# How the reciprocal deviations get from tokens' rows to output rows: two VectorE turns and four small transfers a group, in place of a TensorE product

## The chip, the core and the metric

The kernel runs on one core of a Trainium2 chip. The metric is device microseconds of one execution. The core's engines work from queues of their own, each in the order of the program: TensorE (PE; its weight loads are listed as PEld), VectorE (DVE), ScalarE (ACT), GpSimd (POOL) and SyncE (SP), which here only issues DMA transfers. ScalarE and GpSimd issue some transfers too. A name with a q behind it (SPq, ACTq) is the engine's sequencer: waits and issues.

## The reference

Two blocks, one after the other. The first filters a sequence in the frequency domain; the second is a feed-forward block with SoLU and a layer norm, all in float32:

```python
X = np.fft.rfft(x, axis=1)                      # x: (8, 3136, 256)
y = np.fft.irfft(X * (filt_r + 1j * filt_i), n=3136, axis=1)
t = y.reshape(25088, 256)
h = t @ w_in                                    # (25088, 1024)
e = np.exp(h - h.max(-1, keepdims=True))
solu = h * e / (e.sum(-1, keepdims=True) + 1e-9)
mu = solu.mean(-1, keepdims=True)
var = ((solu - mu) ** 2).mean(-1, keepdims=True)
out = ((solu - mu) / np.sqrt(var + 1e-6) * g_ln) @ w_out
```

What matters here is the factor 1 / sqrt(var + 1e-6): one number for each of the 25,088 tokens, which multiplies the token's output row.

## The kernel before

**Tiling.** The tokens are cut into 196 blocks of 128, two blocks make a pair (98 pairs), two pairs a group (49 groups of 4 blocks). The loop at the end runs `step(k)` for k = 0 to 204; an even k and the odd one behind it belong to pair j = k // 2. A step holds one block's work in each of several stages, so that the engines work on different blocks at once: the hidden product (`product`, L799, seven products for a pair of blocks instead of eight, with sums of blocks made by GpSimd), its evacuation by ScalarE (`keep`, L809) and VectorE (`finish`, L823 and L820), two and three steps later the exponential (L833), the normalization (L845), the turn (L863) and the variance (L853), and some five pairs later the output product (`project`, L935) and its scaling (`keep_out`, L951 on ScalarE; `finish_out`, L955 on VectorE). The Fourier transforms of the next batch elements are spread over the same steps: rows of x are loaded three steps ahead (L270), multiplied (L294, L326, L396), and go through DRAM between.

**Order.** Everything is inside `tc.manual_schedule()`: each engine runs its instructions in the order in which `step` issues them. Semaphores are set by the framework.

**Turn and regroup.** The output product needs the hidden dimension on the partitions. VectorE's transpose works on squares of 32x32. `turn(k)` (L863) transposes a block's 128x1024 in such squares, and `regroup(p, i)` (L880) moves 32-row strips of four turned blocks together with four transfers of 128 KB on SyncE's queue, into the tile `solu_t`. By this the tokens come out in another order: the token at partition 32a + i of block b of a group is row 32b + i of output tile a.

**The factor's way.** ScalarE leaves the four blocks' variances in a tile of 128 x 4. `deviations(g)`, at step k = 4g + 6, computes rs = (var + floor) ** -0.5 on GpSimd (L890, L891). This has the token's partition 32a + i on the rows and the block b in the columns, and must become row 32b + i, column a. So GpSimd also writes `wide` (L893), a 128 x 128 tile in which each rs stands in the column of its place in the square of 32, and at k = 4g + 8 `regroup_deviations` lets TensorE multiply it by a table of 128 x 4 that picks the square (L899), into a corner of a PSUM bank that the output product of the pair before is using (`places`). ScalarE copies the 128 x 4 result to `rs_t` (L902). The first use of it is `keep_out` at k = 4g + 9, then `finish_out`, for the two pairs of the group.

**Queues.** On SyncE, an even step k issues eight transfers of `regroup` (pair j - 3: four for each half), then two stores of output rows (L963), then, in the stages with row loads, four loads of x (L270). `regroup`'s second half reuses the buffer of the pair two before, which TensorE must have read for the last time (`project(p, 4)` in the same step).

Of the kernel before, what the change touches and what calls it, by code (L numbers as in the profile page):

```python
# [9 lines left out]
FP32 = mybir.dt.float32  # L10
# [3 lines left out]
ALU = mybir.AluOpType  # L14
# [4 lines left out]
P = 128  # L19
# [89 lines left out]
def kernel(  # L109
# [10 lines left out]
    nc = tc.nc  # L120
# [6 lines left out]
    de_dram = nc.inline_tensor(de_host, name="de_tbl").ap()  # L127
    there_dram = nc.inline_tensor(
        np.ascontiguousarray(de_host[:, :, 0].reshape(NP, P, P).transpose(1, 0, 2)), name="there_tbl").ap()
    one_dram = nc.inline_tensor(np.eye(P, dtype=np.float32), name="one_tbl").ap()  # L130
    rows = np.arange(P)[:, None]
    turn_dram = nc.inline_tensor(np.concatenate(
        [rows % 32 == np.arange(32), rows // 32 == np.arange(4)], 1).astype(np.float32),
        name="turn_tbl").ap()

    def pool(name, bufs, space=None, stack=ctx):
        kw = {} if space is None else {"space": space}
# [5 lines left out]
    small = pool("sm", 4)  # L143
# [15 lines left out]
    neg_half, floor_sb = small_consts[:, 0:4], small_consts[:, 4:5]  # L159
# [278 lines left out]
    with ExitStack() as st:  # L438
# [145 lines left out]
        for i0, n, rows in ((0, 4, P), (4, 4, P), (8, NP - 9, P), (NP - 1, 1, NQ)):  # L584
            f, at = filters[i0]
# [91 lines left out]
    def psum(name):  # L677
        return ps_t.tile([P, 2, C], FP32, name=name, tag="t")
# [15 lines left out]
    pools["de"] = pool("de1", 2)  # L694
    spread = pool("spread", 1)
    turn_t = spread.tile([P, 36], FP32, name="turn_t", tag="turn_t")
    second.pools = pools
    for c, at, n, kind, dims in (
            (0, 0, 4 * C, "t2", "p (v c) -> p v c"), (0, 4 * C, 4 * C, "f", "p (v k c) -> p v k c"),
# [188 lines left out]
    def deviations(g):  # L888
        rs = small.tile([P, 4], FP32, name=f"rs_{g}", tag="rs", bufs=2)
        nc.gpsimd.tensor_tensor(out=rs, in0=variances.pop(g), in1=floors.pop(g), op=ALU.add)  # L890
        nc.gpsimd.tensor_tensor(out=rs, in0=rs, in1=neg_half, op=ALU.pow)  # L891
        spreads[g] = wide = spread.tile([P, 4, 32], FP32, name=f"wide_{g}", tag="wide")
        nc.gpsimd.tensor_tensor(  # L893
            out=wide, in0=turn_t[:, 0:32].rearrange("p (o i) -> p o i", o=1).broadcast_to([P, 4, 32]),
            in1=rs.rearrange("p (b o) -> p b o", o=1).broadcast_to([P, 4, 32]), op=ALU.mult)

    def regroup_deviations(g, ps):

        nc.tensor.matmul(out=ps, lhsT=spreads.pop(g).rearrange("p b i -> p (b i)"), rhs=turn_t[:, 32:36],  # L899
                         start=True, stop=True)  # L900
        rss[g] = small.tile([P, 4], FP32, name=f"rs_t_{g}", tag="rs_t")
        nc.scalar.copy(out=rss[g], in_=ps)  # L902

    def project_sums(p, step):

# [146 lines left out]
    def step(k):  # L1052
        j, odd = divmod(k, 2)
        p = j - (LAG - 1) // 2 if odd else j - (LAG + 1) // 2
        if not 0 <= p < pairs:
            p = None
        hid, proj = k < blocks, p is not None
        sums_of_x = differences[k] + products[k]
        if not odd and k > LAG:
            for job in sums_of_x:  # L1060
                job()
            sums_of_x = []
        if not odd and 2 <= j - 4 < pairs:
            project_sums(j - 4, 0)
        if k < LAG:
            if not odd:
                product(j, 1)
                keep(j, k, 0)
                product(j, 2)
                finish(j, k, 0, (k, 0), 1)  # L1070
            else:
                product(j, 5)
                keep(j, k - 1, 1)
                finish(j, k, 1, (k - 1, 1), 2)
        for job in top[k] + (sums_of_x + stores[k] if k < LAG else stores[k] + sums_of_x):
            job()
        if not odd and 0 <= j - 4 < 2:
            project_sums(j - 4, 0)
        if odd and j + 1 < pairs:
            pair_sums(j + 1)  # L1080
        if not odd:
            if hid and k > LAG:
                product(j, 1)
                keep(j, k, 0)
            if 2 <= k < blocks:
                exponential(k - 2)
            if proj:
                project(p, 5)
                keep_out(p, 1, (1, 1) if p in last else (0, 1))
            if p in last:  # L1090
                keep_out(p, 0, (0, 1))
                finish_out(p, 1, 1, (1, 1), 1)
            if blocks <= k < blocks + 2:
                exponential(k - 2)
            if hid and k > LAG:
                product(j, 2)
            if 3 <= k < blocks + 3:
                turn(k - 3)
            if hid and k > LAG:
                finish(j, k, 0, (k, 0), 1)  # L1100
            if proj and p not in last:
                finish_out(p, 1, 1, (0, 1), 1)
            for job in early[k]:
                job()
            if 3 <= k < blocks + 3:
                square(k - 3)
            if hid:
                product(j, 6)
                keep(j, k + 1, 0)
            if proj:  # L1110
                project(p, 3)
                if p not in last:
                    keep_out(p, 0, (0, 1))
                project(p, 4)
            if j >= 4 and j % 2 == 0 and j - 4 < pairs:
                regroup_deviations((j - 4) // 2, places.pop(p) if proj else psum("ps_rs")[:, 0, 0:4])
            for job in spectrum_loads[k]:
                job()
            if 0 <= j - 3 < pairs - 2:
                regroup(j - 3, 0)  # L1120
                regroup(j - 3, 1)
            elif j - 3 == pairs - 2:
                regroup(j - 3, 1, nc.scalar.dma_start, range(2))
                regroup(j - 3, 0)
                regroup(j - 3, 1, parts=range(2, 4))
                regroup(j - 2, 0)
                regroup(j - 2, 1, parts=range(2))
            if 0 <= j - 4 < pairs:
                project_sums(j - 4, 1)
            if j - 3 == pairs - 2:  # L1130
                regroup(j - 2, 1, nc.gpsimd.dma_start, range(2, 4))
            if 0 <= j - 3 < pairs and j % 2:
                deviations((j - 3) // 2)
            if hid:
                product(j, 7)
            if p in last:
                finish_out(p, 0, 1, (0, 1), 2)
                finish_out(p, 1, 0, (1, 0), 1)
                store_out(p)
            if 2 <= k < blocks + 2:  # L1140
                normalize(k - 2)
            for job in second_parts[k] + middle[k] + first_parts[k]:
                job()
            if proj and p not in last:
                finish_out(p, 1, 0, (1, 0), 1)
                store_out(p)
        else:
            if hid and k >= LAG:
                product(j, 5)
                keep(j, k - 1, 1)  # L1150
                finish(j, k, 1, (k - 1, 1), 2)
            for job in early[k]:
                job()
            if proj:
                project(p, 1)
                keep_out(p, 0, (0, 0))
                project(p, 2)
                finish_out(p, 0, 0, (0, 0), 1)
            if 2 <= k < blocks + 2:
                exponential(k - 2)  # L1160
            if hid:
                product(j, 3)
                product(j, 4)
            if proj:
                project(p, 6)
                project(p, 7)
            for job in second_parts[k] + middle[k]:
                job()
            if 3 <= k < blocks + 3:
                turn(k - 3)  # L1170
            if hid:
                finish(j, k - 1, 1, None, 0)
                finish(j, k, 0, (k, 0), 2)
            if 2 <= k < blocks + 2:
                normalize(k - 2)
            if proj:
                keep_out(p, 1, (1, 0))
            if 3 <= k < blocks + 3:
                square(k - 3)
            for job in first_parts[k]:  # L1180
                job()
        if k < 3:
            convert_w_out(k + 1)
        if k == 2:
            prepare_w_out(0)
        if k == 4:
            prepare_w_out(1)
        if 5 <= k < 9:
            prepare_w_out(k)
        for job in late[k] + loads[k]:  # L1190
            job()
        if k < 4:
            scale_w_out(k)

    with tc.manual_schedule():
        pair_sums(0)
        nc.gpsimd.dma_start(out=turn_t, in_=turn_dram)
        for load in first_loads:
            load()
        nc.vector.tensor_scalar(out=g_sb, in0=g_sb, scalar1=-1.0 / SHRINK, scalar2=None, op0=ALU.mult)  # L1200
        convert_w_out(0)
        for k in range(blocks + LAG):
            step(k)
# [30 lines left out]
```

## Time and profile before

| | |
|---|---|
| median of 3 runs | 1576.14 us (1568.17 to 1578.04) |
| the profiled execution | 1569.28 us, span 1567.5 us |
| granted TensorE clock, mean | 0.996 |
| PE busy | 1532.5 us (98%), 12844 matmul passes |
| DVE busy | 1254.9 us (80%) |
| POOL busy | 1157.2 us (74%) |
| ACT busy | 927.9 us (59%) |
| DMA, share of 16 engines: SyncE's queue, GpSimd's, ScalarE's | 42.5%, 18.6%, 7.2% |

A float32 product is carried out in two passes, so 49 products L899 are 98 matmul passes and 98 weight loads. A line of the profile's groups gives line, engine, operation, out<-in by the program's names, shape and count, and behind the bar the busy time and the mean of one in ns. In the views by time the first number is the start in us from the start of the span, the second the length; merged instructions carry a count (x8). `[0.75 <-ACT rs_t L902]` means that the engine was idle for 0.75 us before, and that ScalarE's instruction of line 902 ended this. The transfers are busiest up to 1200 us (DMA share 0.71 to 0.81 in the stretches of 120 to 300, 300 to 600, 600 to 1060 and 1060 to 1200 us) and quiet behind (0.43 from 1200 to 1520 us), when no Fourier work is left.

### The profile page before, as it was taken

The numbers are of one execution on the slowest core, as the hardware profiler recorded it, in microseconds if no ns is written. First come the engines' busy times: TensorE is split into PE (matmuls) and PEld (weight loads), VectorE is DVE, ScalarE is ACT, GpSimd is POOL, SyncE is SP. The second block draws the span as 40 slices with busy tenths as digits, with TensorE's granted clock in tenths as the row PEclk, the third lists the DMA queues.
The fourth block names the chain that finished last, engine by engine and source line by source line (L and its number), as shares of the span: only waits on it lengthen the run. The fifth ranks groups of instructions, "written<-read, shape, count | busy, mean of one in ns | idle before, by whom it ended". The sixth has DMA issues, their size and how long they took to land.

```text
span 1567.5 us, 36719 instructions
## 1 busy us (share of the span) xinstructions
PE 1532.5 (98%) x12844; PEld 1061.7 (68%) x12844; DVE 1254.9 (80%) x2233; ACT 927.9 (59%) x1898; POOL 1157.2 (74%) x1346
## 2 busy tenths in 40 slices
PE   8988999999999999999999999999999999999997
PEld 5633576667666776667766776667776777777777
DVE  4879878897998789878998698877998777776773
ACT  3565655666556656666566655666556666666663
POOL 2578886697879678887779767786766767676665
PEclk9999999999999999999999999999999999999999
DMA  9768788877987689667886588766874545343434
GB/s 246 252 202 226 218 225 220 227 212 207 252 242 204 173 236 254 196 173 192 249 230 190 152 229 247 203 184 176 233 204 119 138 122 135 88 115 102 116 104 118
DMA packets 342256, 298.07 MB, mean 190 GB/s; under 512 B 27915, under 2 KB 311573, under 8 KB 342073
## 3 DMA queue, kind: packets, MB, share of 16 engines
q1 hardware_dynamic: 278872, 175.82, 42.5%
q0 software_dynamic: 29568, 87.33, 18.6%
q10 hardware_dynamic: 33634, 32.58, 7.2%
q8 instruction: 104, 1.70, 0.5%
q14 instruction: 78, 0.64, 0.1%
HBM read 118.02 MB, written 74.84 MB: 123 GB/s over the span
## 4 chain that ended last, share of the span: by engine, by line
PE 59%; DMA 2%; DVE 0%; SPq 0%; issue 0%; POOL 0%; ACT 0%; ACTq 0%; POOLq 0%
PE o L935 26%; PE m L799 26%; PE py L396 2%; PE pc L326 1%; PE pa L294 1%; PE pb L326 1%; DMA solu_t<-turn 1%; DMA x<-in_x_dram 0%; SPq L880 0%; DMA out_dram<-ot 0%; PE o L899 0%; POOL u L778 0%; ACT e L833 0%; DVE h L845 0%; DVE h L820 0%
## 5 line engine op out<-in xcount | busy, mean ns | idle before, releaser
L935 PEld LDWEIGHTS o<-w_out_sb,solu_t 128*128 128x128 f32 x3136 | 381.1, 192 | 47.3 <-issue 43.5
L799 PE MATMUL m<-w_in_sb,s 128*128 128x512 f32 x784 | 398.4, 609 | 5.8 <-ACT h L809 3.3
L935 PE MATMUL o<-w_out_sb,solu_t 128*128 128x128 f32 x3136 | 400.2, 276 | 1.7 <-DVE ot L955 1.6
L935 PEld LDWEIGHTS o<-w_out_sb,u 128*128 128x128 f32 x2352 | 306.4, 191 | 138.3 <-issue 108.6
L799 PE MATMUL m<-w_in_sb,y 128*128 128x512 f32 x588 | 307.8, 607 | 5.6 <-DVE nmax L823 3.8
L935 PE MATMUL o<-w_out_sb,u 128*128 128x128 f32 x2352 | 309.6, 275 | 2.6 <-POOL u L778 1.8
L845 DVE SCALAR_TENSOR_TENSOR h<-e,h 128x1024 f32<-128x1024 f32 x196 | 308.7, 1575 | 0.4 <-ACT e L833 0.4
L951 ACT ACTIVATE ot<-o,rs_t 128x128 f32<-128x128 f32 x392 | 143.6, 367 | 248.2 <-PE o L935 246.1
L809 ACT COPY h<-m 128x512 f32<-128x512 f32 x294 | 173.2, 589 | 195.6 <-PE m L799 191.0
L778 POOL TENSOR_TENSOR u<-solu_t 128x512 f32<-128x512 f32 x98 | 135.0, 1377 | 184.7 <-DMA solu_t<-turn 126.2
L823 DVE CUSTOM_DVE_ANT_0 h<-m,h 128x512 f32<-128x512 f32 x196 | 134.3, 685 | 165.4 <-ACT h L809 103.1
L853 ACT ACTIVATE h<-h,nmu 128x1024 f32<-128x1024 f32 x196 | 225.1, 1148 | 53.4 <-DVE turn L863 53.4
L863 DVE STREAM_TRANSPOSE turn<-h 128x1024 f32<-128x1024 f32 x196 | 243.0, 1240 | 3.8 <-DVE ot L955 0.3
L833 ACT ACTIVATE e<-h,nmax 128x1024 f32<-128x1024 f32 x196 | 225.3, 1149 | 8.1 <-DVE h L845 6.6
L778 POOL TENSOR_TENSOR u<-solu_t,u 128x512 f32<-128x512 f32 x98 | 136.0, 1388 | 94.0 <-PE o L935 93.4
L799 PEld LDWEIGHTS m<-w_in_sb,s 128*128 128x128 f32 x784 | 127.9, 191 | 90.9 <-issue 71.6
L955 DVE SCALAR_TENSOR_TENSOR ot<-o,rs_t,ot 128x128 f32<-128x128 f32 x299 | 103.7, 347 | 97.0 <-ACT ot L951 59.8
L778 POOL TENSOR_TENSOR u<-u,solu_t 128x512 f32<-128x512 f32 x98 | 161.9, 1652 | 15.9 <-PE o L935 9.0
L799 PEld LDWEIGHTS m<-w_in_sb,y 128*128 128x128 f32 x588 | 96.7, 191 | 102.1 <-issue 46.2
L778 POOL TENSOR_TENSOR solu_t<-solu_t,solu_t 128x512 f32<-128x512 f32 x98 | 155.0, 1581 | 0.9
L778 POOL TENSOR_TENSOR s<-y 128x128 f32<-128x128 f32 x196 | 100.2, 511 | 6.1 <-DMA x<-in_x_dram 5.7
L396 PEld LDWEIGHTS py<-wb_t,t 50*64 50x64 f32 x3584 | 57.6, 135 | 42.9 <-issue 18.7
(121 smaller groups left out, 1953.9 us busy)
## 6 DMA issues: line engine op xcount, KB each, us to landing
solu_t<-turn SPq DMA_DIRECT2D x780, 128.0 KB
out_dram<-ot SPq DMA_DIRECT2D x196, 128.0 KB
t<-d POOLq DMA_DIRECT2D x112, 200.0 KB, 6.8
d<-x POOLq DMA_DIRECT2D x100, 200.0 KB, 5.3
t<-d ACTq DMA_DIRECT2D x37, 512.0 KB
f<-f_dram POOLq DMA_DIRECT2D x37, 512.0 KB, 7.6
d<-g POOLq DMA_DIRECT2D x36, 512.0 KB, 5.0
x<-in_x_dram SPq DMA_DIRECT2D x112, 98.0 KB
```

What stands on the lines that cost most here:

```text
L396: nc.tensor.matmul(out=views[g][64 * h:64 * h + 64, cb, i, :], lhsT=t4[rows, i, c0:c0 + 64], rhs=wb_t[rows, 0:N1], start=True, stop=True)
L778: nc.gpsimd.tensor_tensor(out=out, in0=in0, in1=in1, op=op)
L799: nc.tensor.matmul(out=ms[j, bank], lhsT=lhsT, rhs=w_in_sb[:, w, :], start=m in (1, 2, 7), stop=True, skip_group_check=True)
L809: nc.scalar.copy(out=h_half(k, i), in_=ms[j, 0])
L823: nc.vector.tensor_tensor_reduce(out=h_half(k, i), in0=ms[j, bank], in1=h_half(*kept), scale=1.0, scalar=sofar, op0=ALU.add, op1=ALU.min, ...
L833: nc.scalar.activation(out=e, in_=hs[k], func=AFT.Exp, bias=nmaxs.pop(k)[:, 1:2], scale=-1.0, accum_out=esums[g][:, i:i + 1])
L845: nc.vector.scalar_tensor_tensor(out=solu, in0=e, scalar=SHRINK, in1=solu, op0=ALU.mult, op1=ALU.mult, accum_out=nmu)
L853: nc.scalar.activation(out=solu, in_=solu, func=AFT.Square, bias=nmu, scale=-float(DFF), accum_out=variances[g][:, i:i + 1])
L863: nc.vector.transpose(out=turns[g][:, :, i, :], in_=solus[k].rearrange("p (f j) -> p f j", j=32))
L935: nc.tensor.matmul(out=pos[p, bank], lhsT=lhs[:, f, :], rhs=w[:, f, :], start=f == 0 and (m in (1, 2, 7) or alone), stop=True, skip_group_ ...
L951: nc.scalar.activation(out=out_half(p, *to)[0], in_=pos[p, 0], func=AFT.Copy, scale=rs)
L955: nc.vector.scalar_tensor_tensor(out=ot, in0=pos[p, bank], scalar=rs, in1=out_half(p, *kept)[0], op0=ALU.mult, op1=ALU.add)
```

## The change

The product by TensorE goes, but for the last group. GpSimd now writes rs into the first four columns of a tile `lines` of 128 x 32. At the end of step 4g + 7 VectorE turns `lines` in its squares of 32, in place: rs of block b and square a then lies along row 32a + b. Four transfers on SyncE's queue move these rows, four rows of 32 numbers (128 bytes) each, to the rows a, 32 + a, 64 + a, 96 + a of `corners`, and at the end of step 4g + 8 VectorE turns `corners` in place: row 32b + i, column a holds what is wanted. `corners` has two halves, one for even and one for odd groups; `lines` is one buffer. Both are set to zero once at the start. The last group (g = 48) still uses `wide`, the product and ScalarE's copy. A constant table's place in DRAM moves as well.

```diff
+    lines = small.tile([P, 32], FP32, name="lines", tag="lines", bufs=1)
+    corners = spread.tile([P, 2, 32], FP32, name="corners", tag="corners")
...
     def deviations(g):
...
-        nc.gpsimd.tensor_tensor(out=rs, in0=rs, in1=neg_half, op=ALU.pow)
-        spreads[g] = wide = spread.tile([P, 4, 32], FP32, name=f"wide_{g}", tag="wide")
-        nc.gpsimd.tensor_tensor(
-            out=wide, in0=turn_t[:, 0:32].rearrange("p (o i) -> p o i", o=1).broadcast_to([P, 4, 32]),
-            in1=rs.rearrange("p (b o) -> p b o", o=1).broadcast_to([P, 4, 32]), op=ALU.mult)
+        nc.gpsimd.tensor_tensor(out=lines[:, 0:4], in0=rs, in1=neg_half, op=ALU.pow)
+
+        if 2 * g == pairs - 2:
+            spreads[g] = wide = pools["diff"].tile([P, 4, 32], FP32, name=f"wide_{g}", tag="diff")
+            nc.gpsimd.tensor_tensor(
+                out=wide, in0=turn_t[:, 0:32].rearrange("p (o i) -> p o i", o=1).broadcast_to([P, 4, 32]),
+                in1=lines[:, 0:4].rearrange("p (b o) -> p b o", o=1).broadcast_to([P, 4, 32]), op=ALU.mult)
+
+    def product_deviations(g, ps):
...
-        rss[g] = small.tile([P, 4], FP32, name=f"rs_t_{g}", tag="rs_t")
+        rss[g] = corners[:, g % 2, 0:4]
         nc.scalar.copy(out=rss[g], in_=ps)
+
+    def regroup_deviations(g):
+
+        places = corners[:, g % 2, :]
+        nc.vector.transpose(out=lines, in_=lines)
+        for a in range(4):
+            nc.sync.dma_start(out=places[a:P:32, :], in_=lines[32 * a:32 * a + 4, :])
+
+    def place_deviations(g):
+
+        rss[g] = places = corners[:, g % 2, :]
+        nc.vector.transpose(out=places, in_=places)
...
-            if j >= 4 and j % 2 == 0 and j - 4 < pairs:
-                regroup_deviations((j - 4) // 2, places.pop(p) if proj else psum("ps_rs")[:, 0, 0:4])
+            if k == blocks + 4:
+                product_deviations(pairs // 2 - 1, places[p])
...
+        if k >= 7 and k % 4 == 3 and k - 3 < blocks:
+            regroup_deviations((k - 7) // 4)
+        if k >= 8 and k % 4 == 0 and k - 4 < blocks:
+            place_deviations((k - 8) // 4)
         if k < 3:
             convert_w_out(k + 1)
...
+        nc.gpsimd.memset(lines, 0.0)
+        nc.gpsimd.memset(corners, 0.0)
```

The two new calls stand at the end of a step, behind its evacuations, normalization and spectrum products and ahead of `late[k]` and of the step's loads.

More of the change, by code (lines that the diff above doesn't have):

```diff
@@ L129 @@
         np.ascontiguousarray(de_host[:, :, 0].reshape(NP, P, P).transpose(1, 0, 2)), name="there_tbl").ap()
-    one_dram = nc.inline_tensor(np.eye(P, dtype=np.float32), name="one_tbl").ap()
     rows = np.arange(P)[:, None]
@@ L134 @@
         name="turn_tbl").ap()
+    one_dram = nc.inline_tensor(np.eye(P, dtype=np.float32), name="one_tbl").ap()
     def pool(name, bufs, space=None, stack=ctx):
@@ L890, in deviations @@
         nc.gpsimd.tensor_tensor(out=rs, in0=variances.pop(g), in1=floors.pop(g), op=ALU.add)
-        nc.gpsimd.tensor_tensor(out=rs, in0=rs, in1=neg_half, op=ALU.pow)
-        spreads[g] = wide = spread.tile([P, 4, 32], FP32, name=f"wide_{g}", tag="wide")
-        nc.gpsimd.tensor_tensor(
-            out=wide, in0=turn_t[:, 0:32].rearrange("p (o i) -> p o i", o=1).broadcast_to([P, 4, 32]),
-            in1=rs.rearrange("p (b o) -> p b o", o=1).broadcast_to([P, 4, 32]), op=ALU.mult)
-    def regroup_deviations(g, ps):
-        nc.tensor.matmul(out=ps, lhsT=spreads.pop(g).rearrange("p b i -> p (b i)"), rhs=turn_t[:, 32:36],
+        nc.gpsimd.tensor_tensor(out=lines[:, 0:4], in0=rs, in1=neg_half, op=ALU.pow)
[5 more added lines that the diff above has]
+    def product_deviations(g, ps):
+        wide = spreads.pop(g)
+        nc.tensor.matmul(out=ps, lhsT=wide.rearrange("p b i -> p (b i)"), rhs=turn_t[:, 32:36],
                          start=True, stop=True)
-        rss[g] = small.tile([P, 4], FP32, name=f"rs_t_{g}", tag="rs_t")
+        rss[g] = corners[:, g % 2, 0:4]
         nc.scalar.copy(out=rss[g], in_=ps)
+    def regroup_deviations(g):
[6 more added lines that the diff above has]
+        nc.vector.transpose(out=places, in_=places)
     def project_sums(p, step):
```

## The prediction

> **What bounds the kernel.** I read the chain of work that ended last first, since it says on which engine a saved microsecond shortens the run. By engine (shares of the span):
>
> ```profile
> PE 59%; DMA 2%; DVE 0%; SPq 0%; issue 0%; POOL 0%; ACT 0%; ACTq 0%; POOLq 0%
> ```
>
> Nearly all that it attributes is TensorE. Then the same chain in order of time, around one of the products that the change removes (start, length, what):
>
> ```profile
> 1383.49 1.78 PE o L935 x16
> 1385.28 0.12 PE o L899 x2
> 1385.40 1.82 PE m L799 x4
> 1387.22 1.78 PE o L935 x16
> 1389.01 1.72 PE m L799 x4
> ```
>
> Matmul follows matmul without a hole, and the product (L899) stands in the row: 0.12 us of its own, and the four L799 matmuls behind it take 1.82 instead of 1.72. So its price is about 0.22 us of pure path. Next, VectorE's instructions there (start, length, ..., idle time before it and who ended it):
>
> ```profile
> 1380.57 0.08 DVE L845 DVE_READ_ACCUMULATOR h<-e,h 128x1 f32 x1
> 1380.69 1.25 DVE L863 STREAM_TRANSPOSE turn<-h 128x1024 f32<-128x1024 f32 x1
> ...
> 1385.63 0.35 DVE L955 SCALAR_TENSOR_TENSOR ot<-o,rs_t,ot 128x128 f32<-128x128 f32 x1 [0.75 <-ACT rs_t L902]
> 1387.88 0.69 DVE L823 CUSTOM_DVE_ANT_0 h<-m,h 128x512 f32<-128x512 f32 x1 [1.90 <-ACT h L809]
> ```
>
> The first new turn will stand between L845 and L863 (1380.65), the second behind L955 (1386.0), where VectorE idles 1.90 us today. The time between them, 5.3 us here, is all that the four transfers have. Then SyncE's queue:
>
> ```profile
> 1376.24 1.30 SPq L963 DMA_DIRECT2D out_dram<-ot  x2
> 1377.65 3.03 SPq L880 DMA_DIRECT2D solu_t<-turn  x4
> ```
>
> These four L880 transfers are issued 3.0 us before VectorE reaches the first turn; behind the change they stand after the new ones. Last, the chain where it leaves TensorE, at the end and in the row-loading stage, since its DMA pieces give the time from issue to landing:
>
> ```profile
> 978.17 9.80 DMA solu_t<-turn
> ...
> 988.38 6.36 DMA x<-in_x_dram
> ...
> 1531.40 0.13 PE o L899 x2
> 1531.54 0.48 SPq L880
> ...
> 1533.39 2.49 DMA solu_t<-turn
> ```
>
> On quiet queues a 128 KB transfer lands in 2.49 us, on full ones in up to 9.80; and at the end the regrouping of pair 95 is itself on the path.
>
> **Removed from TensorE.** 49 products, one kept: 48. From the last L935 matmul ahead to the third L799 pass behind takes 1.195 to 1.196 us in all 44 cases with a whole record, and 0.972 in the median of 167 passages without the product: 0.224 us. 48 x 0.224 = **10.8 us**, on the path. One rule of the Trainium skill ("TensorE: Matmul & The Clock Gate", section "Step-by-step: what each phase is for") says that the next weights load while the running matmul streams. By it the loads would be hidden and only the 0.12 us would go, 5.8 us in all; the trace disagrees, as a four-column matmul covers no load (two loads, 0.11 us apart), and the row decides.
>
> **Removed elsewhere.** GpSimd loses the L893 product (49 x 402 ns), ScalarE the copy L902 (0.16 us, with a wait of 25.7 us in all for L899), VectorE's L955 its wait for L902 (19.8 us in 25 cases). None of these three engines is in the chain; I count nothing, and keep a gain for the rivals.
>
> **Added on VectorE.** 96 turns of 128x32. No such row exists. L863's 128x1024 took 1.245 us and never stretched (1226 to 1248 ns over 196), so 1/32 of it is 0.04 us; the shortest VectorE instruction takes 0.08. Between 0.04 and 0.12 I take 0.1. The first turn delays L863, which has idle time behind it (0.85 us in the view above). The second is uncovered in the 16 of 47 groups in which VectorE's next instruction starts without a gap: 16 x 0.1 = **1.6 us**; with no cover at all, 9.6.
>
> **The new wait: second turn on the four transfers.** Behind it on VectorE stand L279 and L823, and TensorE's next products wait for L823 (32.9 us in 44 cases today); ScalarE's first scaling of the pair (L951) waits for the turn itself, 2.2 us later in most groups, 0.3 in a few. For each of 47 groups I took from the trace: the end of L845 (first turn), the last SyncE issue ahead, and the start of VectorE's next instruction behind L955. The time available has a median of 7.4 us (3.4 to 9.5). The transfers are issued at the first turn's end, or when SyncE is free, or when their semaphore is: by the waits in the trace, the transfers of SyncE and ScalarE take turns on eight semaphores, and each issue waits until the transfer eight before has landed. Issue cost: 4 packets each; SyncE's shortest row is 0.28 us (L270), its usual one 0.63; below 0.28 it can go to 0. I take 0.28. Landing: no tiny transfer is in the trace. I take the 2.49 us of the quiet regrouping, and not before all transfers issued ahead have landed, as they share the queue. The ends are 2.49 without a change, 4.82 (median of L880 from 600 to 1060 us, loaded) and 9.80. Summed over the groups, beyond the idle time behind: **2.6 us** (groups 1, 5, 9, 27, 47); with issues of 0 to 0.66, 2.4 to 4.4; with 4.82 in the loaded stage, 22 to 30; with 9.80 there, 155. Until pow (L891) is done the first turn would wait too, but that ends at least 3.8 us ahead.
>
> **Moved: SyncE's regrouping.** L880 of the second pair of a group now waits for VectorE: its first half is issued 2 to 7.5 us later. That half alone is of no use to GpSimd, whose first sum needs the second half, and the second half waits for TensorE anyway (4.65 us after the first turn in the view above; four transfers of 0.28 and four of 0.65 end at 3.8). Over all groups the second half starts 14.7 us later in sum, at most 2.0 in one; from its landing to TensorE's first use pass 3.5 us or more, so this is hidden, except in group 47: its regrouping is in the chain shown, **1.9 us** onto the end. Row loads and stores behind L880 move by as much; they are issued three steps ahead.
>
> **The sum.** -10.8 + 1.6 + 2.6 + 1.9 = -4.7 us on the profiled execution: 1569.3 to 1564.6. That execution was 6.9 us under the median of the runs (1576.1), so **1571 us** there. About 1% (16 us) is what a measurement of this kernel can tell from no change, and this is within it.
>
> **Rivals.** (1) *Slower: the transfers land late where the queues are full.* Place: the second turn in groups 4 to 29. For it: in the row-loading stage five to eight of the eight semaphores are in use at the first turn, the third and fourth transfer wait for stores and rows issued 6 to 10 us before, and the chain shows 9.80 and 6.36. Against: a tiny one has no data of its own to wait for. It decides from a landing of about 4.5 us there; price 22 to 30 us, so +14 to +22: 1591 to 1598 us. The Trainium skill ("DMA: Bandwidth & Descriptors", section "Why a DMA increments its semaphore by 16 and not by 1") has a rule for it: a transfer whose slowest dimension is four rows runs on the four lowest-numbered engines, as row loads of 49 rows run on the lowest seven; no row here names a packet's engine. Chance 0.22. (2) *Slower still: the four go one after another,* if writes to interleaved rows of one tile count as overlapping. Four times 2.49 is 10 us against 7.4 available; summed in the same way with 9.2, the waits come to 154 to 177 us: about 1740. Nothing in the trace has such rows. Chance 0.08. (3) *Faster by more than 1%: the freed waits reach TensorE.* L955 without its 19.8 us of waiting, and GpSimd 0.4 us a group earlier; if half of the 19.8 gets through and the new waits stay covered, -10.8 - 9.9 + 1.9 = -19: 1557. Against: the chain hardly touches these engines. Chance 0.15. (4) *The change doesn't deliver:* the next matmul then waits for something else and only the costs remain, +6: 1582. Against: the unbroken row of matmuls. Chance 0.05.
>
> **Chances and range.** The forecast has 0.50, with a range of its own of 1565 to 1580. Faster by over 1%: 0.15; within: 0.50 + 0.05; slower: 0.22 + 0.08. 1556 to 1600 leaves out (2) and the tails of (1) and (3).
>
> **What will show it.** In the chain, L935 followed at once by L799 at 1.72 us. The second turn without idle time before it, or, if (1) holds, with waits for DMA of 1 to 3 us in groups 4 to 29 and L823 late behind; if (2), such waits in every group, to the end. L880 starting right behind the first turn and its second half where it was. The last stretch 1 to 2 us longer. Wrong is the prediction if the waits for these transfers sum to over 10 us, or if TensorE's passage behind L935 doesn't shrink by 0.2 us.

## The result and the profile after

The changed kernel takes **1578.93 us** in the median of 12 runs (1574.98 to 1582.05), the kernel before 1573.04 us in the median of 12. The ratio is **1.0038, 95% interval 1.0021 to 1.0055**: slower by some 6 us, within the 1% that was called no change, but clearly on the other side of the forecast of 1571 us. The profiled execution took 1574.98 us, span 1573.1 us, against 1569.28 and 1567.5 before: +5.6 us of span, where the sum of the prediction was -4.7.

TensorE did what was forecast. The chain of work that ended last, in order of time, in the changed kernel (start, length, what), around the place of the removed product; L935 is now L952, L799 is L801:

```profile
1385.43 0.86 PE m L801 x2
1386.29 0.89 PE o L952 x8
1387.18 1.72 PE m L801 x4
1388.90 1.86 PE o L952 x16
1390.76 1.72 PE m L801 x4
```

The output product is followed at once by the next hidden product, which takes 1.72 us; the piece of 1.82 is gone. Next VectorE there (start, length, instruction, idle time before it and who ended it):

```profile
1361.54 0.20 DVE L912 STREAM_TRANSPOSE lines<-lines 128x32 f32<-128x32 f32 x1
1361.67 1.23 DVE L865 STREAM_TRANSPOSE turn<-h 128x1024 f32<-128x1024 f32 x1
...
1366.20 0.35 DVE L972 SCALAR_TENSOR_TENSOR ot<-o,corners,ot 128x128 f32<-128x128 f32 x1 [0.43 <-PE o L952]
1366.47 0.20 DVE L919 STREAM_TRANSPOSE corners<-corners 128x32 f32<-128x32 f32 x1
1368.54 0.69 DVE L825 CUSTOM_DVE_ANT_0 h<-m,h 128x512 f32<-128x512 f32 x1 [1.86 <-ACT h L811]
```

In this quiet group the second turn waits for nothing, and L825 behind it still waits 1.86 us for ScalarE, so the turn costs nothing here. It takes 0.20 us, not 0.1. SyncE's queue near the end of the same stage (start, length, instruction, count):

```profile
1381.13 1.30 SPq L980 DMA_DIRECT2D out_dram<-ot  x2
1387.19 2.28 SPq L914 DMA_DIRECT2D corners<-lines  x4
1389.56 4.68 SPq L882 DMA_DIRECT2D solu_t<-turn  x7
```

The regrouping (L882) starts right behind the four transfers, as forecast. The four take 2.28 us of SyncE's queue, 0.57 each, where 0.28 was taken. All second turns, by their source line:

```profile
L919 DVE STREAM_TRANSPOSE corners<-corners x48: 194/202/214, 147.8 to 1538.0; 128x32 f32<-128x32 f32 x48
...
  DMA corners<-lines: 19.2, 13
```

13 of 48 wait for the transfers, 19.2 us in all, and a 14th, in group 26, waits 2.3 us that this list puts down to another transfer (below): 21.5 us in 14 cases, longest in groups 9 (4.1), 28 (3.6), 1 (3.3) and 26 (2.3). The last of them starts at 1062 us. From 1200 us on most of the transfers land 1.0 us after their issue has ended; before 1060 us they need 1.0 to 6.0. The case of group 26, in the chain of the changed kernel:

```profile
954.42 8.37 DMA out_dram<-ot
...
962.81 0.02 SPq L914
...
962.86 5.16 DMA corners<-lines
...
968.04 3.79 DMA de<-de_tbl
971.83 0.05 DVE corners L919
```

The first transfer of L914 can't be issued until a store of output rows has landed, 8.37 us after the store's issue began, since both count on the same one of eight semaphores. The second waits in the same way for the other store. By the trace the fourth is issued only at 967.38 us and lands at 971.70, and the turn starts at 971.8. (The chain's table load, `de<-de_tbl`, is only the next transfer on the first one's semaphore; the turn does not need it.) And the profile of waits (who waited for whom: us in total, times, longest). First the kernel before, then the changed one:

```profile
POOL u L778 <- DMA solu_t<-turn: 126.2, 43, 7.4
...
PEld m L799 <- DVE nmax L823: 32.9, 44, 2.9
...
DVE diff L279 <- DMA x<-in_x_dram: 5.4, 5, 2.1
```

```profile
POOL u L780 <- DMA solu_t<-turn: 177.1, 57, 8.1
...
PEld m L801 <- DVE nmax L825: 41.5, 52, 2.9
...
DVE corners L919 <- DMA corners<-lines: 19.2, 13, 4.1
...
DVE diff L279 <- DMA x<-in_x_dram: 9.4, 7, 2.3
...
ACT h L811 <- DMA solu_t<-turn: 9.3, 3, 3.7
```

There are two candidates here. One is the new wait itself, with what stands behind it. The other is the line on top: GpSimd waits 51 us more for the regrouping, and ScalarE's evacuations (L811) stand behind ScalarE's own transfers, whose issue is held, which they hardly did before. L279 is VectorE's difference of two sets of x rows; it needs the row loads (L270) and stands right behind the second turn in 20 of the 48 groups. The experiments separate the candidates.

**Where on the time axis.** I cut both spans at the start of VectorE's normalization (L845, L847 after) of the first block of a group, and compare the lengths of the stretches; in brackets the idle time of TensorE, in us:

| groups | before | after minus before | without the transfers (below) minus before |
|---|---|---|---|
| 0 to 3 | 132.3 (11.1) | +2.6 (+4.3) | +0.2 (+2.8) |
| 4 to 9 | 192.5 (1.9) | -1.1 (0.0) | -1.8 (-0.2) |
| 10 to 17 | 252.7 (1.6) | +3.3 (+4.5) | -2.6 (-0.3) |
| 18 to 23 | 181.8 (0.0) | +3.6 (+3.1) | -1.6 (0.0) |
| 24 to 29 | 182.6 (0.6) | +0.7 (+1.4) | -1.8 (-0.2) |
| 30 to 35 | 176.4 (0.3) | -1.4 (0.0) | -0.9 (+0.5) |
| 36 to 41 | 159.2 (0.2) | -1.8 (-0.2) | -1.8 (-0.2) |
| 42 to 47 | 148.5 (0.0) | -1.2 (0.0) | -1.3 (0.0) |
| behind | 47.6 (8.5) | +1.4 (+1.8) | +1.6 (+1.8) |

The stretch ahead of group 0 is left out (0.5 us shorter after, 2.2 longer without the transfers). From group 36 on the change saves 3.0 us in 12 groups, 0.25 a group: the 0.224 of the product and a little more. What is lost is lost ahead of that, in the larger part as idle time of TensorE (13.3 us more in groups 0 to 35), but for 1.4 us behind the last group.

### The profile page after: what moved, and what is told of

Its sections match the earlier page's. It is cut to its first block, busy times and chain, and to the rows that moved or that the text cites. A ratio compares the mean times of both kernels' runs of the same rounds, so it can differ in the third digit from the quotient of the medians.

```text
span 1573.1 us, 36938 instructions
## 1 busy us (share of the span) xinstructions
PE 1523.8 (97%) x12748; PEld 1050.9 (67%) x12748; DVE 1254.2 (80%) x2329; ACT 918.6 (58%) x1850; POOL 1135.9 (72%) x1300
## 5 line engine op out<-in xcount | busy, mean ns | idle before, releaser
L952 PEld LDWEIGHTS o<-w_out_sb,solu_t 128*128 128x128 f32 x3136 | 382.0, 192 | 47.5 <-issue 43.3
L801 PE MATMUL m<-w_in_sb,s 128*128 128x512 f32 x784 | 395.3, 605 | 10.8 <-ACT h L811 5.8
L952 PE MATMUL o<-w_out_sb,solu_t 128*128 128x128 f32 x3136 | 401.0, 276 | 1.8 <-DVE ot L972 1.7
L952 PEld LDWEIGHTS o<-w_out_sb,u 128*128 128x128 f32 x2352 | 306.9, 192 | 141.3 <-issue 107.4
L801 PE MATMUL m<-w_in_sb,y 128*128 128x512 f32 x588 | 307.6, 606 | 10.9 <-DVE nmax L825 8.7
L952 PE MATMUL o<-w_out_sb,u 128*128 128x128 f32 x2352 | 310.4, 275 | 5.2 <-ACT ot L968 3.1
L811 ACT COPY h<-m 128x512 f32<-128x512 f32 x294 | 172.9, 588 | 227.4 <-PE m L801 186.9
L780 POOL TENSOR_TENSOR u<-solu_t 128x512 f32<-128x512 f32 x98 | 138.7, 1415 | 230.7 <-DMA solu_t<-turn 177.1
L847 DVE SCALAR_TENSOR_TENSOR h<-e,h 128x1024 f32<-128x1024 f32 x196 | 296.5, 1513 | 0.4 <-ACT e L835 0.4
L968 ACT ACTIVATE ot<-o,corners 128x128 f32<-128x128 f32 x392 | 143.4, 367 | 254.8 <-PE o L952 240.1
L825 DVE CUSTOM_DVE_ANT_0 h<-m,h 128x512 f32<-128x512 f32 x196 | 134.3, 685 | 162.1 <-ACT h L811 96.6
L780 POOL TENSOR_TENSOR u<-solu_t,u 128x512 f32<-128x512 f32 x98 | 139.5, 1424 | 78.2 <-PE o L952 78.0
L801 PEld LDWEIGHTS m<-w_in_sb,s 128*128 128x128 f32 x784 | 128.0, 191 | 97.3 <-issue 85.0
L780 POOL TENSOR_TENSOR u<-u,solu_t 128x512 f32<-128x512 f32 x98 | 165.7, 1691 | 11.0 <-DMA out_dram<-ot 2.4
L972 DVE SCALAR_TENSOR_TENSOR ot<-o,corners,ot 128x128 f32<-128x128 f32 x299 | 103.5, 347 | 85.4 <-ACT ot L968 53.2
L801 PEld LDWEIGHTS m<-w_in_sb,y 128*128 128x128 f32 x588 | 95.6, 190 | 109.0 <-DVE nmax L825 41.5
L780 POOL TENSOR_TENSOR solu_t<-solu_t,solu_t 128x512 f32<-128x512 f32 x98 | 144.8, 1478 | 0.9
L780 POOL TENSOR_TENSOR s<-y 128x128 f32<-128x128 f32 x196 | 103.0, 526 | 5.2 <-ACT y L423 4.7
```

What stands on the lines that cost most here:

```text
L780: nc.gpsimd.tensor_tensor(out=out, in0=in0, in1=in1, op=op)
L801: nc.tensor.matmul(out=ms[j, bank], lhsT=lhsT, rhs=w_in_sb[:, w, :], start=m in (1, 2, 7), stop=True, skip_group_check=True)
L811: nc.scalar.copy(out=h_half(k, i), in_=ms[j, 0])
L825: nc.vector.tensor_tensor_reduce(out=h_half(k, i), in0=ms[j, bank], in1=h_half(*kept), scale=1.0, scalar=sofar, op0=ALU.add, op1=ALU.min, ...
L847: nc.vector.scalar_tensor_tensor(out=solu, in0=e, scalar=SHRINK, in1=solu, op0=ALU.mult, op1=ALU.mult, accum_out=nmu)
L952: nc.tensor.matmul(out=pos[p, bank], lhsT=lhs[:, f, :], rhs=w[:, f, :], start=f == 0 and (m in (1, 2, 7) or alone), stop=True, skip_group_ ...
```

## The experiments

The theories: **W**, the loss is VectorE's wait at the second turn, for transfers that land late (rival 1 of the prediction). **R**, the loss is what the transfers do to the other transfers: SyncE's time, and places in the rotation of eight semaphores that SyncE's and ScalarE's transfers share. **Q**, added later: the small packets slow the DMA engines themselves. Ratios are against the kernel before, with 95% intervals; us are the ratio on 1573 us.

### Without the transfers

```diff
-        for a in range(4):
-            nc.sync.dma_start(out=places[a:P:32, :], in_=lines[32 * a:32 * a + 4, :])
```

> The changed kernel without its four transfers: both turns stay, and the second works on a tile of ones, so the output rows are left unscaled except in the last group (this part of the computation is left out). It gives what the change is worth with its transfers taken away. 48 products at 0.224 us are 10.8 us less on TensorE; 96 turns at the 0.20 us that the changed kernel's profile shows cover themselves in two of three groups and cost 3 us. All theories that believe in the saving: 7 to 10 us under the kernel before. If the product's 0.224 us did not shorten the run (the next matmul waits for something else), within 2 us of the kernel before.

Measured: 0.9932 (0.9920 to 0.9945), -10.7 us by the ratio and -9.7 by the medians. So the saving on TensorE is real and reaches the end. The turns' cost and what the work taken from GpSimd and ScalarE may give are in this number too; it doesn't tell them apart. What the transfers bring with them costs 0.0106 of 1573, **17 us**.

### The transfers into a tile that nobody reads

```diff
-            nc.sync.dma_start(out=places[a:P:32, :], in_=lines[32 * a:32 * a + 4, :])
+            nc.sync.dma_start(out=sink[a:P:32, g % 2, :], in_=lines[32 * a:32 * a + 4, :])
```

> The changed kernel with its four transfers issued from the same place and of the same size, but into a tile that nobody reads; the second turn works on a tile of ones and waits for nothing (the scaling of the output rows is left out, but for the last group). Theory W (the loss is VectorE waiting at the second turn for late transfers, 19.2 us in 13 cases): as without transfers, 6 to 10 us under the kernel before. Theory R (the loss is what the transfers do to the others: they take SyncE's time, 0.50 to 0.57 us each, and four more places in the rotation of eight semaphores, and so hold up ScalarE's own issues, 22.0 us there after against 10.5 before, and the regrouping): between 1 us under and 6 us over the kernel before.

Measured: 1.0063 (1.0047 to 1.0079), +10 us. The waits of this kernel (its profile is of the slowest of six runs, 1590.62 us against a median of 1582.68):

```profile
POOL u L781 <- DMA solu_t<-turn: 181.7, 56, 8.7
PEld m L802 <- DVE nmax L826: 42.5, 56, 2.7
...
DVE diff L279 <- DMA x<-in_x_dram: 18.5, 10, 3.0
...
ACT h L812 <- DMA solu_t<-turn: 14.6, 4, 5.1
```

VectorE no longer waits for the transfers, yet GpSimd's and TensorE's waits are as in the changed kernel, and so is the time, or worse. **Theory W falls.** VectorE has not gained the time: freed at the turn, it waits at L279 for the row loads, 18.5 us against 9.4 in the changed kernel. R had expected -1 to +6; it has the sign, and the size is above it.

### The transfers added to the kernel before

```diff
+    def idle_transfers(g):
+        for a in range(4):
+            nc.sync.dma_start(out=sink[a:P:32, g % 2, :], in_=lines[32 * a:32 * a + 4, :])
...
+        if k >= 7 and k % 4 == 3 and k - 3 < blocks:
+            idle_transfers((k - 7) // 4)
```

> The kernel before, product kept and all that is computed the same, plus the four transfers of each group at the place that they have in the changed kernel, from a tile of zeros into a tile that nobody reads: no turns, no wait. Theory W: 0 to 2 us over the kernel before. Theory R: 7 to 14 us over it, with ScalarE's issues held for some 20 us instead of 10, and TensorE's losses at the same kind of place (the row-loading stage, up to 1060 us).

Measured: 1.0195 (1.0173 to 1.0218), **+31 us**, more than twice what R had allowed for, from transfers of 512 bytes that nobody waits for. By stages, +29.2 us up to group 35, of these 18.0 as idle time of TensorE, and -0.5 in groups 36 to 47. The top of its waits:

```profile
POOL u L780 <- DMA solu_t<-turn: 181.7, 58, 9.1
```

The same 182 us as with the sink. The cost per transfer is larger here than in the changed kernel, and why isn't settled.

### One transfer and eight

```diff
-        for a in range(4):
+        for a in range(1):
```

and, in the other kernel, `range(8)` with each of the four issued twice, to both halves of the sink.

> The kernel before plus one idle transfer of four rows per group on SyncE instead of four. With 30 us for four: theory R with a loss per transfer gives 5 to 10 us over the kernel before. If the loss comes from which large transfer stands eight places behind which (the phase of the rotation), it is not in proportion: anything from 5 under to 20 over.

> The kernel before plus eight idle transfers of four rows per group on SyncE, twice the four. Eight is a whole turn of the eight semaphores, so every large transfer keeps the semaphore that it has in the kernel before. A loss per transfer gives 50 to 75 us over the kernel before; a loss from the phase of the rotation alone gives under 15 us.

Measured: one 1.0078 (1.0048 to 1.0108), +12 us; eight 1.0412 (1.0386 to 1.0438), +65 us. One, four and eight give 12, 31 and 65: a loss per transfer, though not quite in proportion. The phase of the rotation alone is out, as eight are a whole turn of it. With eight, by stages, +70.7 us of span up to group 35 (51.7 idle) and -0.3 in groups 36 to 47. GpSimd's wait goes on rising, and VectorE's for the row loads rises more steeply:

```profile
POOL u L780 <- DMA solu_t<-turn: 229.5, 60, 10.1
...
DVE diff L279 <- DMA x<-in_x_dram: 68.6, 17, 7.2
```

### Issued by GpSimd

```diff
-            nc.sync.dma_start(out=sink[a:P:32, g % 2, :], in_=lines[32 * a:32 * a + 4, :])
+            nc.gpsimd.dma_start(out=sink[a:P:32, g % 2, :], in_=lines[32 * a:32 * a + 4, :])
```

> The kernel before, product kept, everything computed, plus the four idle transfers per group of the run with added transfers, at the same place in the order, but issued by GpSimd instead of SyncE. GpSimd's transfers count on semaphores of their own, so neither SyncE's time nor the rotation of eight semaphores is touched; the bytes and packets are the same. Theory R (SyncE's queue and its rotation carry the loss): 0 to 8 us over the kernel before, what there is coming from GpSimd's own issue time, four times 0.53 us a group. Theory Q (the small packets disturb the DMA engines, whoever issues them): 20 to 35 us over, as with SyncE.

Measured: 1.0092 (1.0064 to 1.0119), +14 us: half of what the same transfers cost on SyncE, between what R and Q expected. A part of Q can't be excluded: the regrouping's second half needs 5.4 us from its last issue to landing (mean of pairs 2 to 59), against 4.8 in the kernel before. The rest may be GpSimd's own 0.56 us per issue; I have not separated the two. GpSimd's wait for the regrouping, 116.2 us, is here under the 126.2 of the kernel before, so that wait doesn't follow the time.

The Trainium skill ("DMA: Bandwidth & Descriptors", section "Issuing engines are not separate DMA queues") says that all issuers' transfers run on the same 16 engines, and that another issuer saves only sequencer time, "which is usually small relative to the DMA itself". For transfers of 512 bytes the trace doesn't agree with "small": 0.57 us of issue against 1.0 us to landing in the quiet groups, and a change of issuer halved the loss.

### The changed kernel with GpSimd's transfers and an earlier first turn

```diff
         finish_out(p, 0, 0, (0, 0), 1)
+            if k >= 7 and k % 4 == 3 and k - 3 < blocks:
+                regroup_deviations((k - 7) // 4)
...
-            nc.sync.dma_start(out=places[a:P:32, :], in_=lines[32 * a:32 * a + 4, :])
+            nc.gpsimd.dma_start(out=places[a:P:32, :], in_=lines[32 * a:32 * a + 4, :])
```

> The changed kernel, everything computed, with the four transfers issued by GpSimd, and the first turn about 4 us earlier in VectorE's order (behind the finished output half of the odd step, when pow has been done for 0.5 us or more), so that GpSimd issues them in its idle time before the next sums. Theory R: the saving of 9.7 us without transfers stays but for GpSimd's 2.1 us a group where its sums are waited for, 2 to 9 us under the kernel before. Theory W (late transfers are waited for at the second turn): as the changed kernel, 4 to 8 us over, since GpSimd's transfers do not land sooner. Theory Q: 5 to 20 us over.

Measured: 0.9982 (0.9968 to 0.9997), **-2.8 us**, as R said. By its source line, the transfers' instruction and who waited for it:

```profile
L914 POOL DMA_DIRECT2D corners<-lines x192: 560/562/677, 138.8 to 1523.3; - x192
...
  DVE corners L919: 0.6, 2
```

The second turn waits 0.6 us in all. And GpSimd's wait for the regrouping is 92.1 us, under the 126.2 of the kernel before.

### Earlier, but still on SyncE

The first hunk of the last diff alone.

> The changed kernel with one line moved: the first turn and its four transfers, still on SyncE, about 4 us earlier in the order (behind the finished output half of the odd step). Everything computed. The transfers then have 4 us more to land, and SyncE is held less long for the first turn (133 us in the changed kernel's profile). Theory W, or the hold of SyncE's queue behind the first turn: 3 to 9 us under the kernel before. Theory R (issue time and places in the rotation, wherever they stand): 3 us or more over it.

Measured: 1.0033 (1.0019 to 1.0046), +5 us, as R said and as the changed kernel itself. Two of its waits, VectorE's and then, from SyncE's own list, what held the transfers:

```profile
DVE corners L919 <- DMA corners<-lines: 15.7, 9, 3.9
```

```profile
SPq L914 <- DMA out_dram<-ot: 31.5, 33, 2.4
```

SyncE no longer waits for the first turn (133.4 us in the changed kernel), so the order behind that wait was not the cause either. Instead the transfers wait for stores to land, on the shared semaphores, and 4 us more to land in save only 3.5 us of the second turn's waits.

### Behind the regrouping

The idle transfers of the added run, moved to the end of the next, even step:

```diff
-        if k >= 7 and k % 4 == 3 and k - 3 < blocks:
-            idle_transfers((k - 7) // 4)
+        if k >= 8 and k % 4 == 0 and k - 4 < blocks:
+            idle_transfers((k - 8) // 4)
```

> The kernel before plus the four idle transfers per group on SyncE, but at the end of the next, even step, behind that step's regrouping and stores instead of ahead of a regrouping. Everything computed. If the loss is SyncE's issue time, 2.2 us, standing directly ahead of a regrouping: 0 to 12 us over the kernel before. If it is the places in the rotation, which are the same wherever they stand: 20 to 35 us over.

Measured: 1.0182 (1.0155 to 1.0209), +29 us, as at the other place and in the range expected of the rotation. It doesn't rule out the issue time: here the four stand directly ahead of row loads, so that these are issued later (in one group, by the trace, the transfers take SyncE from 614.6 to 618.7 us and the loads start at 618.9).

### In the quiet groups only

The product kept in groups 0 to 29 and 48, turns and transfers in 30 to 47:

```diff
+    def by_turns(g):
+        return 30 <= g < pairs // 2 - 1
```

> The turns and transfers only in groups 30 to 47, where no rows are loaded any more; groups 0 to 29 and 48 keep the product. Everything is computed. Both theories: 18 products at 0.224 us are 4.0 us less, the end is 1.3 us later by the last stretch of the two profiles, so 2.7 us under the kernel before (1 to 4.5). If the loss sits in the quiet groups as well: at or over the kernel before.

Measured: 0.9996 (0.9983 to 1.0009), -0.6 us, and the interval reaches from -2.7 to +1.4. By stages groups 36 to 47 save 2.7 us, and the stretch behind the last is 1.8 longer. That the transfers cost nothing in the quiet groups is borne out by the stages; the whole time alone doesn't show it.

### Both together

GpSimd's transfers and the early first turn in groups 0 to 33, the changed kernel's own way in 34 to 46, the product in 47 and 48:

```diff
-            nc.sync.dma_start(out=places[a:P:32, :], in_=lines[32 * a:32 * a + 4, :])
+            (nc.gpsimd if g < 34 else nc.sync).dma_start(out=places[a:P:32, :], in_=lines[32 * a:32 * a + 4, :])
...
-        if 2 * g == pairs - 2:
+        if g >= pairs // 2 - 2:
```

> Everything computed. Groups 0 to 33: the four transfers issued by GpSimd, first turn 4 us earlier (as in the run with GpSimd's transfers); groups 34 to 46: the changed kernel as it is, transfers on SyncE; groups 47 and 48: the product. Theory R (the transfers cost only where SyncE's queue is full, and nothing in the quiet groups): against the kernel before, the stages up to group 36 give 6 us as in the profile with GpSimd's transfers, groups 36 to 47 3 us as in the profile without transfers, the end nothing: 6 to 10 us under it. If GpSimd's gain there was chance, or the quiet groups cost on SyncE after all: 0 to 4 us under.

Measured: **0.9972 (0.9957 to 0.9987), -4.4 us**: the fastest of the kernels that compute everything, though short of the 6 to 10 expected. Its interval and that of GpSimd's transfers everywhere overlap. By stages it keeps 3.1 us in groups 36 to 47, but only 0.4 in 0 to 35, and the stretch behind is 2.9 us longer though the product stands there again.

### What goes through SyncE

For each kernel I took from the trace how late the last transfer of a pair's regrouping was issued, counted from the same earlier turn (mean of pairs 2 to 59, relative to the kernel before), how long it then took to land, how much SyncE and ScalarE waited before 1060 us with an issue ready but for the landing of the transfer ahead on its semaphore, and how long VectorE waited for transfers at the second turn and at L279. "Cost" is the time by the ratio, above the kernel before where the product is kept, above the run without transfers where it isn't.

| kernel | issue later by, us | issue to landing, us | waits for a semaphore's last transfer, us | VectorE's waits for transfers, us | cost, us |
|---|---|---|---|---|---|
| before | 0 | 4.8 | 147 | 5.8 | 0 |
| no transfers | 0.0 | 4.7 | 142 | 7.5 | 0 |
| changed | 1.6 | 4.5 | 162 | 30.9 | 17 |
| changed, into the sink | 2.2 | 4.7 | 172 | 20.9 | 21 |
| changed, earlier | 1.2 | 4.6 | 182 | 22.5 | 16 |
| before + one | 1.3 | 5.2 | 170 | 24.8 | 12 |
| before + four | 2.9 | 4.8 | 208 | 37.0 | 31 |
| before + four, behind | 2.5 | 4.9 | 182 | 32.4 | 29 |
| before + eight | 5.8 | 4.1 | 240 | 72.1 | 65 |
| before + four on GpSimd | 0.8 | 5.4 | 155 | 16.9 | 14 |
| changed, on GpSimd, earlier | 0.0 | 5.0 | 139 | 3.6 | 8 |

The column of semaphore waits depends on how "ready" is reckoned: two other reckonings differ from it by up to 31 us (131 and 169 for the changed kernel), so it sets only the kernels with four and eight added transfers clearly apart.

With transfers on SyncE the time follows the lateness of the regrouping's issue, some 10 us of time per 1 us, while its landing time doesn't grow in proportion (4.1 us with eight). The row loads, too, land no later after their issue: 6.2 us before, 5.6 with four added, 5.3 with eight (means of the loads issued from 230 to 1060 us). This points to what happens before the issue, not to the DMA engines. The lateness is also fed by the slower run itself, since the second half waits for TensorE to free a buffer.

The way to TensorE can be read in part. In the kernel before, the last row load of a set lands 2.4 us ahead of VectorE's L279 in the mean (39 sets from 230 to 1060 us), so there is little to lose, and L825, for which TensorE's next hidden product waits, follows L279 at once in 43 of 48 cases. Among the kernels with added transfers VectorE's waits rise roughly with the cost. Of TensorE's holes of over 0.1 us in groups 0 to 35, 28.7 us in the changed kernel against 15.4 before, 6.0 end with an instruction of VectorE that follows such a wait within 3.5 us (0.6 before), 3.7 with ScalarE's L811 behind idle time (none before), and only 0.4 with GpSimd's L780, whose wait is the one that grew most. With eight added transfers 34.0 of 67.1 us stand behind L279's wait. Part of the holes isn't traced to anything, and the 8 us of the last row are not VectorE's waits.

Whether SyncE's 2.2 us of issuing a group or the four places in the rotation weigh more is **open**: every transfer brings both, and the two places tried in SyncE's order cost the same.

## Why the prediction was wrong

**Removed from TensorE, 10.8 us: right.** The stretches show 0.25 us a group where nothing disturbs, and without transfers the time fell by 10.7 us by the ratio; that this comes so near to 10.8 is partly luck, as the turns and the work taken from other engines are in it. The estimate of 5.8 us by the rule of the Trainium skill weighed there ("TensorE: Matmul & The Clock Gate", section "Step-by-step: what each phase is for") lies below that interval (8.6 to 12.6 us); the row was the better guide.

**Added on VectorE, 1.6 us: mis-sized per turn, and too small to see in the time.** The turn takes 0.20 us, over the 0.12 of the upper bound, since a 128x32 transpose is not 1/32 of a 128x1024 one: 0.20 against 1.24. Without transfers VectorE's next instruction starts without a gap behind 17 of the 48 second turns (16 of 47 were forecast), so 3.4 us is an estimate of the cost; the 10.7 us with its interval of 2 us either way allow it and don't show it.

**The new wait, 2.6 us: mis-sized, and no cost of its own.** It measured 21.5 us, in 14 groups instead of five: the issue took 0.57 instead of 0.28, the landing 1.0 to 6.0 us in the loaded groups instead of 2.49, and issues were held by the semaphores. Rival 1 had nearly this number (22 to 30) and, but for group 1, the right place. But its mechanism isn't the cause: with the second turn freed of the wait, no time came back.

**Moved, SyncE's regrouping, counted as hidden: this is the step that failed.** It followed the issues of one group in the quiet part, found 3.8 us of work within 4.65 us of slack, summed 14.7 us of delay for the second halves over all groups and wrote it off. Measured, the last issue of a pair's regrouping is 1.6 us later in the mean of the 58 loaded pairs (between 1.7 earlier and 7.7 later), 93 us in sum. The 3.5 us and more that were to cover it, from landing to TensorE's first use, are not free: GpSimd's sums stand in between, and wait 51 us longer, though hardly any of that shows in TensorE's holes. What does show comes from the sentence that let the row loads and stores go as "issued three steps ahead": their landing had 2.4 us to spare in the mean, and VectorE's waits at the second turn and at L279 together rose from 5.8 to 30.9 us. ScalarE's table loads were not counted at all. They share the eight semaphores; up to 1060 us ScalarE's issues were held for 18.8 us by the landing of the transfer ahead, against 4.9 before, with its evacuations queued behind them. The price of the transfers was 17 us on the path, where the sum had 2.6 us for the wait and nothing for this step but 1.9 at the end, and it was 21 us in the kernel in which the turn waits for nothing.

**The end, 1.9 us: not settled.** The stretch behind group 47 is 1.4 us longer, but also 1.6 us longer without the transfers, and 2.9 in the last kernel of the experiments, which has neither turns nor transfers for groups 47 and 48. The end of the chain, from the last long row of matmuls to the one that ends the run:

```profile
1530.96 6.48 PE o L952 x56
...
1550.19 3.14 DMA solu_t<-turn
...
1557.38 10.54 PE o L952 x88
```

From the first row's end (1537.44) to the last row's start pass 19.9 us; before, 1531.54 to 1551.66, 20.1. The regrouping did not lengthen this.

**The chances.** Slower by over 1% had 0.30 and within 1% 0.55, and the time lay within the range. That it lay within the range owes something to luck: the range was wide enough for a rival whose mechanism isn't the cause. What failed is the sign: the sum had one large certain gain and put nearly every cost of the transfers on the one engine that waits for them.

## What to carry to other kernels

Price a small transfer by what it does to its queue: an issue of half a microsecond and a semaphore held until it has landed, both ahead of whatever is issued next, however few bytes it has and whoever waits. Then look for the transfers behind it that land with the least to spare; here these were the row loads. Where a queue is loaded, test that alone: add the transfers to the old kernel, into a tile that nobody reads, and their price stands by itself. And slack read in a quiet stage doesn't hold in a loaded one; take it in the stage in which the issues are densest.

## What the runs showed of the hardware

- A transfer of four rows of 128 bytes costs SyncE 0.50 to 0.61 us of issue (185 of 192 in the changed kernel) and mostly lands 1.0 us behind it on quiet queues. On GpSimd the issue takes 0.56 us, and the transfer lands 4.8 us after its start in the median (1.8 to 7.4).
- The transfers of SyncE and ScalarE of this kernel count on eight semaphores in turn, and an issue waits until the transfer ahead on its semaphore has landed: 8.37 us from a store's issue in the case shown.
- VectorE's transpose of 128x32 float32 takes 0.20 us, of 128x1024 1.24 us.
- TensorE's granted clock was lower in some stretches with holes. From the table of stretches (start and end, length, PE busy, matmul passes, granted clock, DMA share, GB/s), first before, then with eight added transfers:

```profile
425.00:680.00 255.00, 253.39 (x2286) 1.00 0.78 217
```

```profile
425.00:680.00 255.00, 240.70 (x2244) 0.97 0.81 209
```

14 us of idle time in 255 came with a clock of 0.97 instead of 1.00. But from 1050 to 1220 us the same run has 9.6 us of idle time in 170 at 1.00, so what sets the clock is not shown.
